# Mirrored weight rows by an indirect gather during the load of x, and by SBUF copies, instead of a reversed copy in DRAM

## The chip, the core and the metric

The kernel runs on one core of one Trainium2 chip. The metric is the device time in microseconds; the kernel before takes 273.87 us in the median of five runs (271.23 to 274.94). The engines of the core are called TensorE (PE; its weight load is PEld), VectorE (DVE), ScalarE (ACT), GpSimd (POOL) and Sync (SP). Sync does no arithmetic: it issues DMAs, in the order of its program.

## What is computed

The input x has 2048 rows of 448 values in bfloat16. Two layers follow one another; each is a global filter (A) and a feed-forward block (B), both with a residual and a layer norm without parameters:

```
def _A_ref(x, w_r, w_i):
    X = rfft2(x.astype(float32), axes=(-2, -1))
    X = X * (w_r + 1j * w_i)              # 2048 x 225 complex weights
    return irfft2(X, s=(S, D)).astype(bfloat16)

def _B_ref(x, w1, b1, w2, b2):
    h = x @ w1 + b1                       # 448 -> 1792
    r = where(h > 0, h, 0)
    return (r * r) @ w2 + b2              # 1792 -> 448

x = x + _A_ref(layernorm(x), A_w_r, A_w_i)
x = x + _B_ref(layernorm(x), B_w1, B_b1, B_w2, B_b2)
x = x + _A_ref(layernorm(x), A_w_r, A_w_i)
x = x + _B_ref(layernorm(x), B_w1, B_b1, B_w2, B_b2)
```

The same filter weights w_r and w_i serve both layers.

## The kernel before

**The filter as matmuls.** x lies in SBUF as 16 tiles of 128 rows (`x_raw`, `x_sb`). The transform over 2048 rows is split into a part over 32 and a part over 64 positions. Stage A (`first_A`, line 774) does the first part, tile by tile: layer norm statistics (`ln_stats`, line 731), a copy of the mirrored second half of x (`xr`, lines 684 to 686), the transform matrix scaled by the inverse deviation (`Fs`), five matmuls, and an evacuation from PSUM to `XA`. All 16 tiles must be through A before the next stage. Then come, over the nine groups of frequencies in `GROUPS` (line 24), four stages: TD (transform along the 448 columns, line 793), evacuated to `U`; B (the 64-part, line 814, with the matrices `G_sb`), evacuated to `EF`; W (the weights, on VectorE, line 829), which writes `Z`; and Bi (the inverse 64-part, line 847, with `H_sb`), evacuated to `VT`. `U`, `EF` and `Z` are parts of the tensor `arena`, and so is `b1r`, where the bias b1 lands. TI and AI are the last inverse parts; they and the feed-forward block follow tile by tile (`ffn`, line 1083).

**The weights in SBUF.** Stage W multiplies by two tensors, `Wa` and `Wb`. They live in the memory of `xin` and `yT`, which hold normalised rows and their transpose during the feed-forward block, so the profile calls them xin and yT. Each has 33 blocks of 225 columns (`WC`) on 128 partitions. Partitions alternate between rows of w_r and rows of w_i; `Wb` has the two parts swapped (`W[i ^ f::2]`). Blocks 0 to 16 are rows of the weights as they lie in DRAM. Blocks 17 to 32 are rows of the other half of the spectrum, in reversed order over the partitions ("mirrored rows"). Stage W of group (1,) needs block 1 and block 32.

**Where the mirrored rows come from.** Lines 676 to 678 copy the upper half of each group of 32 rows, for w_r and for w_i, into a DRAM scratch `Wrev` with the groups reversed, 16 x 64 rows of 450 bytes for each. `load_W` (line 689) loads a range of either tensor: two DMAs for the plain blocks and two from `Wrev` for the mirrored ones. It is called for Wa and Wb, for a first and a second range of frequencies (`RANGES`, line 25), and again at lines 1138 to 1141 for layer 2, since the feed-forward block has overwritten them by then.

**Who orders the work.** All instructions are recorded with modelled costs and then put in order by a list scheduler (`_Sched.schedule`, line 307): each unit has a priority, which is the length of the modelled chain behind it plus a bias from the table `PR` (line 115), by stage, layer and group. The table `EN` (line 116) says which engines an evacuation, a copy or a scaling may run on (a is ScalarE, d VectorE, p GpSimd, the other letters a choice of these); the scheduler takes one. Within a queue the initial DMAs keep the order in which they are recorded (`sch.chain`, line 670). On Sync that is: x in five pieces (line 672), Wrev twice, TD, then for the first range G, Wa, Wb, H, J and b1 (lines 699 to 707), then for the second range G, Wa, Wb and H. Only FA goes by ScalarE's queue (line 671). Then come the late loads (line 710), which wait for one group of `U`: matrices of the last stages, the feed-forward weights, b2. A DMA that waits for an event holds up everything behind it on its queue.

**Small things.** GpSimd clears a part of `Z` (line 683) and writes `ones` (line 679); with `ones` TensorE runs dummy matmuls (line 1147) wherever the scheduler finds gaps[...]. `b1_columns` (line 721) turns b1 into a column with one matmul against `J_sb` and a VectorE copy.

Of the kernel before, what the change touches and what calls it, by code (L numbers as in the profile page):

```python
# [10 lines left out]
P = 128  # L11
# [14 lines left out]
WC = 225  # L26
# [88 lines left out]
PR = {'TD': [[1459729, 1259808, 1256228, -3108200, -3115463, -3359604, -3126041, -3425431, 1074746], [2520683, -882130, 2513278, 1403817, -946609, -1006157, -1079382, -1083072, 1408461]], 'B': [[1237773, 1050720, 1249483, 1207627, -3305020, -3131895, -3380703, -3131879, -3405365], [2513805, -1004943, 1405526, 2514030, 1385417, -1091018, 967616, -1128168, -974908]], 'W': [[1253039, 1078572, 1237053, 1034800, 903280, 1085367, 1237103, 1077859, 864382], [258958, 196705, -32086, -31831, 199273, -68617, -58145, -231565, -289839]], 'Bi': [[-3488292, -3416654, -3131052, 3604675, 3610720, 3611807, 3612729, 3611813, -3301256], [-1103789, 969189, -981009, 1254540, 970491, 1105225, 1552262, 1255862, 1105109]], 'ln': [[923936, 825492, 38979, -60850, -37351, -57698, -179414, -623263, 911016], [-271548, -172641, -867906, -1299696, -1320737, -1236672, -1088818, -1447761, -1447490]], 'TI': [[3619976, 3632657, -3289350, -3332308, 3495818, -3359644, -3382949, -3414332, 3519280], [1261769, 1520394, -1042615, -960154, -1117170, -1090629, 1004310, 1104983, -956137]], 'AI': [[4634856, 3460927, 3455093, 3457451, 3466064, 3457816, 4635449, 4511391, 4582726], [-1052212, 1009347, -1087268, -918268, 922485, 1002479, -1037023, 968706, 962689]], 'xb': [[-9860, 798649, -72029, -73353, -90047, -409254, -607363, -507705, 928714], [-893728, -411180, -1254094, -1698528, -1387951, -1443371, -1673366, -1302405, -1812411]], 'h': [[3487659, 4652010, 4616526, 4619112, 4279252, -3285016, 4657270], [-1019342, 991342, 978381, 984290, -1370620, -1116942, 970059]], 'o': [[4661274, 3474862, 4512632, 4653567, 4636097, 4526347, 4564327, 4535148, 4512085, 4508609, 3950179, 3692114, 3696435, 4495598, 3696450, 3616074], [974079, -1169174, 993521, 1038340, 1009246, 993378, 1005699, -1124270, 998883, -1120813, 996336, -1111884, -1172470, -1092181, 987813, -1358625]], 'A2': [[-72035, 284724, -512615, -580766, 929799, -602369, -46361, -576264, 286964, 286775, 286081, 263197, -46145, 286915, -45242, 261493]], 'A1': [[-779, 1247740, 1250779, 1248346, 1246850, 1247319, 1229425, 1230467]], 'aux': [[1178171, 1361770, 1207975, 1470618]], 'A1x': [[77129, -557721, -161592, 998558, 1237344, 1250337, 1172287, -364362]], 'A1f': [[1236079, 88644, 10154, 1243572, 1069050, 1242682, 1242298, 1245995]], 'A1m': [[1247229, 1244654, 1232513, 1232515, 1232520, 1233784, 1090466, 1090451]], 'A1e': [[91431, 1262114, 1234063, 821447, 1226285, 1050805, 1202378, 1161214]], 'A2f': [[-66167, -58636, -509981, -604863, -46624, -51134, -65898, 91768, -45472, 282466, -800266, 262425, -50208, 187315, -808565, -41160]], 'A2s': [[261559, -869540, -630612, -577929, 87311, -116879, -611112, -5940, 190215, -5765, 140813, 56793, 142295, -803032, 255003, 284498]], 'A2m': [[4542048, 3987428, 3994225, 3994222, 4572260, 3668875, 4538774, 3956827, 3571174, -1111431, 1402630, -891134, -1110561, 1395497, 1402686, 1403856]], 'A2e': [[-590800, 320887, 286230, 188640, -45373, -70277, 332615, 191914, -90624, -52362, 212173, 30004, -86939, 123899, -676333, 212918]], 'TDe': [[1232797, 1033581, 1154642, 1278733, 910181, 1202635, 884503, 865587, 1171272], [234287, 1417255, 495995, 497071, -692296, -708408, 116793, 481473, -31496]], 'Be': [[1200284, 1164674, 1131653, 1169731, 847780, 910804, 858910, 875738, 764326], [-673471, -562228, -700927, 509333, -668554, 482845, -571588, -638456, -610624]], 'Ws': [[1121940, 1017298, 877937, 1032459, 1071284, 902054, 1033802, 894050, 1203015], [212971, -52164, -46639, -245211, -58995, -232137, -245502, -184844, -32998]], 'Bie': [[916036, 852841, 889310, 787021, -7275, 912434, 20519, 815367, 892886], [1425225, 487576, -647465, -980124, -655085, -74395, -74265, -181695, -980116]], 'TIe': [[984358, 928435, 897342, -482262, -48765, -430781, 660660, 817396, 914899], [-281201, -65231, -282303, -289086, -289168, -715848, -279815, -281401, -129383]], 'AIf': [[-3552, -92775, -329502, 40139, 70612, 12525, -118916, -459850, -116926], [-493364, -1130841, -1393844, -459441, -971123, -1107764, -912857, -1318923, -1108227]], 'AIs': [[86761, 782322, 38289, 6120, 64218, -59055, -459688, -181931, 53487], [-268252, -1086758, -871049, -882940, -1366310, -1105429, -921449, -1316086, -1362286]], 'lnq': [[216007, -824667, -30202, -469940, -549631, -29481, 10194, -106170, -63028], [-1301120, -1525322, -1460274, -1354285, -1518321, -1584492, -282120, -1317624, -1311702]], 'lny': [[134655, 81887, 30689, -60625, -63986, -78551, 54758, -622412, -65538], [5687, -408331, -899111, -1240287, -1321630, -1511641, -1102623, -1489541, -1703014]], 'fl': [[3485031, 3484724, -3492741, 4199187, 4682003, 4593201, 4541514, -3167665, 4085732], [-1027343, -1036111, -999372, -1485712, 986133, -1257709, -1086255, 916561, 1055334]], 'fle': [[905334, -49032, 934732, -36098, -136978, -622183, -570281, 25108, -505182], [-306736, -824319, -951824, -1361677, -380305, -946687, -1019748, -866050, -219706]], 'hA': [[-91316, -94830, -804496, -803653, -613427, -30062, -46967], [-269918, -1324305, -1361165, -1320271, -1328874, -1558623, -269889]], 'hD': [[57549, -446183, -809038, -509961, -437101, -809519, -103640], [-906097, -1805974, -1432344, -1761489, -1721726, -1363125, -1284385]], 'oD': [[26793, -111208, -638756, -125186, -585807, -75004, 60726, -67909, -4895, -507284, -62475, -418670, 272545, -37450, -48441, 261019], [-1030248, -948113, -1221985, -1677027, -1690921, -1311510, -1733759, -1579025, -1728934, -1777603, -1665476, -1642112, -1777768, -1724124, -1625446, -1379584]]}  # L115
EN = {'lny': ['baadaaddd', 'bbdababdb'], 'A1x': ['rbrpparp'], 'A1f': ['xxpprqdx'], 'A1e': ['baadbbab'], 'A2s': ['adabbddababaabdd'], 'A2e': ['bdadbaadabbadaaa'], 'TDe': ['abdaaabab', 'abadaaaad'], 'Be': ['abababbab', 'abaaabaaa'], 'Bie': ['bababbbbb', 'aaaaabbda'], 'TIe': ['bdbaabaaa', 'aabaabbba'], 'fle': ['aabdbaddb', 'bdbddbddd']}
# [389 lines left out]
def bass_interleave_layers__spectral_gfnet__dense_activation_squared_relu__prompt_kernel(nc, A_x, A_w_r, A_w_i, B_x, B_w1, B_b1, B_w2, B_b2, out):  # L506
# [4 lines left out]
    sch = _Sched()  # L511

    with ExitStack() as es:
# [152 lines left out]
        out_dram = out.rearrange("b (p t) d -> p (b t) d", t=NT)  # L666
        memset(warm[:, 0:1], 1.0)
# [3 lines left out]
        dma("act", FA_sb[:], dc["FA"])  # L671
        for e, a, b in (("sp", 0, 2), ("sp", 2, 4), ("sp", 4, 8), ("sp", 8, 12), ("sp", 12, 16)):
            dma(e, x_sb[:, a:b, :], x_dram[:, a:b, :], slow=1.5)
        w_dram = [w.rearrange("(q k) l -> q (k l)", k=32) for w in (A_w_r, A_w_i)]
        Wrev = nc.dram_tensor("Wrev", (2, 64, 16 * WC), BF16, kind="Internal").ap()
        for i in range(2):
            dma("sp", Wrev[i].rearrange("q (c e) -> c q e", c=16),
                w_dram[i][::-1, 16 * WC:32 * WC].rearrange("q (c e) -> c q e", c=16), writes=[f"Wrev{i}"], slow=1.5)
        memset(ones[:], 1.0, eng="pool")
        sch.warm_deps = [sch.last_write[k] for k in _pages(ones[:])][:1]  # L680
        sch.warm_from = 1300.0
        sch.cold_until = 8000.0
        memset(Z[:, :, :, LW:256], 0.0, eng="pool")
        for a, b in ((0, 2), (2, 4), (4, 6), (6, 8), (8, 10), (10, 12), (12, 14), (14, 16)):
            at[:] = 0, a // 2
# [13 lines left out]
        for n, (p0, p1) in enumerate(RANGES):  # L699
# [5 lines left out]
            if n == 0:  # L705
                dma("sp", J_sb[:], dc["J"])
                dma("sp", b1r, B_b1.rearrange("(f p) -> f p", p=P))
# [523 lines left out]
```

## Time and profile before

| what | value |
|---|---|
| median of five runs | 273.87 us (271.23 to 274.94) |
| the profiled execution | 270.1 us |
| its span, first to last instruction | 268.3 us |
| granted TensorE clock, mean | 1.000 of full speed |
| first x pieces landed; last x piece landed | 3.5 us; 9.8 us |
| Wrev landed, w_r and w_i | 15.3 and 16.5 us |
| b1 landed | 24.8 us |
| first TD matmul; first W multiplication | 20.9 us; 24.0 us |
| last evacuation of Bi, layer 1 | 45.0 us |
| first TD matmul and last evacuation of Bi, layer 2 | 146.9 us; 168.4 us |

All times in the profile are counted from the start of the span. An instruction row of a timeline reads: start, length, engine, line, operation, output<-inputs, shapes, count, and in brackets how long its engine had been idle before it and what ended that. The chain of waits goes back from the last instruction, at each step to what released it. A row "SPq" is the issue of a DMA on Sync's queue; the time to landing is counted from that issue. In the stretches each engine's busy time is followed by its count of instructions; the DMA share is the mean over the 16 DMA engines and can pass 1 where transfers overlap.

### The profile page before, as it was taken

What the parts mean: (1) busy time and instruction counts of PE and PEld (TensorE: products, weight loads), DVE (VectorE), ACT (ScalarE), POOL (GpSimd) and SP (SyncE); (2) the same over time, 40 slices, a digit from 0 to 9 for tenths busy, and PEclk for the clock granted to TensorE, in tenths of its full rate; (3) what the DMA queues carried; (4) which work ended last, traced back from release to release, by engine and by line L of the source; (5) the groups of instructions that cost most, each with busy time, mean ns of one, the idle gap of its engine ahead of it and who ended that gap; (6) DMA issues with size and microseconds to landing.
All of it is one profiled execution on the core that took longest, in us unless ns stands there. A gap on an engine that the chain in (4) does not pass through costs nothing.

```text
span 268.3 us, 6395 instructions
## 1 busy us (share of the span) xinstructions
PE 256.3 (96%) x2383; PEld 162.1 (60%) x2383; DVE 203.6 (76%) x707; ACT 184.6 (69%) x390; POOL 8.2 (3%) x20
## 2 busy tenths in 40 slices
PE   7987999999999999999999999998999999999996
PEld 2666987686645544445557986775754444554454
DVE  4883896999999998566878999799899755213522
ACT  6875997995886657883647997876979885005700
POOL 2630000000000000000000000000000000000000
PEclk9999999999999999999999999999999999999999
DMA  6999999004932244004000000002233600110011
GB/s 187 219 262 308 401 355 292 4 2 91 175 95 97 42 108 108 2 2 137 1 2 0 2 4 0 4 0 45 55 78 75 98 0 20 34 53 19 0 37 51
DMA packets 26554, 23.25 MB, mean 87 GB/s; under 512 B 18364, under 2 KB 23068, under 8 KB 26396
## 3 DMA queue, kind: packets, MB, share of 16 engines
q1 hardware_dynamic: 26380, 22.78, 31.4%
q8 instruction: 19, 0.31, 0.5%
q10 hardware_dynamic: 144, 0.07, 0.1%
q14 instruction: 11, 0.09, 0.1%
HBM read 17.33 MB, written 2.76 MB: 75 GB/s over the span
## 4 chain that ended last, share of the span: by engine, by line
PE 72%; DMA 9%; ACT 8%; DVE 6%; SPq 3%; issue 1%; DVEq 0%
PE ps L588 72%; DMA Wrev<-in_A_w_i_dram 5%; ACT arena L628 4%; DMA yT<-xin 3%; SPq L583 3%; DVE arena L646 2%; ACT VT L628 1%; DMA arena<-in_B_b_dram 1%; ACT tmp L628 1%; ACT XA L628 1%; DVE tmp L646 1%; DVE xin L655 1%; DVE x_raw L926 0%; DVE st L956 0%; DVE x_raw L928 0%
## 5 line engine op out<-in xcount | busy, mean ns | idle before, releaser
L611 ACT ACTIVATE arena<-ps,b1T 128x512 bf16<-128x512 f32 (+1 forms) x140 | 74.3, 614 | 31.0 <-PE ps L588 30.8
L588 PE MATMUL ps<-yT,W_sb 64*128 64x512 bf16 (+1 forms) x980 | 87.2, 333 | 1.2 <-DMA yT<-xin 0.9
L588 PE MATMUL ps<-W_sb,arena 128*128 128x448 bf16 (+1 forms) x476 | 87.1, 342 | 0.0
L588 PEld LDWEIGHTS ps<-yT,W_sb 64*128 64x128 bf16 x980 | 49.0, 94 | 39.1 <-ACT arena L611 3.7
L588 PEld LDWEIGHTS ps<-W_sb,arena 128*128 128x128 bf16 x476 | 46.0, 98 | 37.4 <-issue 0.8
L646 DVE TENSOR_TENSOR arena<-arena 128x512 bf16<-128x512 bf16 (+1 forms) x140 | 46.9, 365 | 19.1 <-ACT arena L611 19.0
L628 ACT ACTIVATE arena<-ps 128x896 bf16<-128x896 f32 (+1 forms) x33 | 26.5, 893 | 3.9 <-PE ps L588 3.8
L1045 DVE TENSOR_TENSOR x_raw<-ps,arena 128x448 bf16<-128x448 f32 (+1 forms) x23 | 13.3, 580 | 20.8 <-PE ps L588 20.8
L1147 PE MATMUL ps<-ones 128*128 128x512 bf16 x54 | 17.1, 437 | 1.9 <-POOL ones L659 1.9
L628 ACT ACTIVATE VT<-ps 128x512 bf16<-128x512 f32 x29 | 16.7, 661 | 2.4 <-PE ps L588 2.4
L628 ACT ACTIVATE XA<-ps 128x512 bf16<-128x512 f32 x24 | 13.3, 593 | 6.8 <-PE ps L588 6.8
L646 DVE TENSOR_TENSOR arena<-tmp 128x896 bf16<-128x896 bf16 (+1 forms) x32 | 17.2, 587 | 0.2
L588 PE MATMUL ps<-H_sb,arena 128*128 128x128 bf16 x256 | 16.5, 219 | 0.7 <-DVE arena L646 0.4
L728 ACT ACTIVATE VT<-x_raw 128x448 bf16<-128x448 bf16 x24 | 13.7, 576 | 4.9 <-DVE x_raw L928 4.8
L646 DVE TENSOR_TENSOR tmp<-VT 128x224 bf16<-128x224 bf16 (+1 forms) x56 | 16.1, 315 | 0.4
L588 PEld LDWEIGHTS ps<-H_sb,arena 128*128 128x128 bf16 x256 | 14.8, 98 | 2.7 <-DVE arena L646 2.7
L588 PE MATMUL ps<-arena,G_sb 128*128 128x224 bf16 x128 | 14.2, 259 | 0.4 <-ACT arena L628 0.4
L728 ACT ACTIVATE tmp<-x_raw 128x448 bf16<-128x448 bf16 x14 | 8.0, 573 | 8.8 <-DVE x_raw L1041 8.6
L628 ACT ACTIVATE tmp<-ps 128x896 bf16<-128x896 f32 (+1 forms) x16 | 12.6, 853 | 2.0 <-PE ps L588 2.0
L928 DVE SCALAR_TENSOR_TENSOR x_raw<-ps,x_raw 128x448 bf16<-128x448 f32 x24 | 14.0, 614 | 0.0
L588 PEld LDWEIGHTS ps<-arena,G_sb 128*128 128x128 bf16 x128 | 11.9, 98 | 1.4 <-ACT arena L628 1.4
L748 DVE BATCH_NORM_STATS2 st<-x_raw 128x6 f32<-128x448 bf16 (+1 forms) x19 | 10.9, 585 | 0.2 <-DMA x_raw<-in_A_x_dram 0.2
(75 smaller groups left out, 263.1 us busy)
## 6 DMA issues: line engine op xcount, KB each, us to landing
xin<-Wrev SPq DMA_DIRECT2D x8, 225.0 KB, 3.2
yT<-Wrev SPq DMA_DIRECT2D x8, 225.0 KB, 4.4
W_sb<-in_B_w_dram SPq DMA_DIRECT2D x2, 896.0 KB, 11.6
out_dram<-x_raw SPq DMA_DIRECT2D x15, 112.0 KB, 1.7
W_sb<-in_B_w_dram SPq DMA_DIRECT2D x1, 1568.0 KB, 18.2
x_raw<-in_A_x_dram SPq DMA_DIRECT2D x3, 448.0 KB, 6.5
H_sb<-c_H SPq DMA_DIRECT2D x1, 1088.0 KB, 9.4
G_sb<-c_G SPq DMA_DIRECT2D x1, 768.0 KB, 6.5
```

What stands on the lines that cost most here:

```text
L583: return e.dma_start(o, i)
L588: op = sch.add("pe", lambda e: e.matmul(_res(o), lhsT, rhs, start=start, stop=stop, skip_group_check=skip), [lhsT, rhs], [o], cost=max(_fr ...
L611: sch.add("act", lambda e: e.activation(o, _res(i), func, **kw), rd, [o], cost=c)
L628: op = sch.add("act", lambda e: e.activation(o, _res(i), ACT.Copy) if h[0].eng == "act" else e.tensor_copy(o, _res(i)), [i], [o], cost=c[" ...
L646: sch.add(eng, lambda e: e.tensor_tensor(o, _res(a), b, op), [a, b], [o], cost=_free(o) / rate + 69.0)
L655: sch.add(eng, lambda e: e.tensor_scalar(o, i, s1, s2, op0=op0, **kw), rd, [o], cost=_free(o) / 3.84 + 50.0 + (10.0, 80.0, 140.0)[len(rd) ...
L728: sch.add("act", lambda e: e.activation(o, x, ACT.Square, accum_out=sd[:, t, 1:2]), [x], [o, sd[:, t, 1:2]], cost=560.0)
L748: small(lambda e, si=si, xi=xi: e.bn_stats(si, xi), [xi], [si], _free(xi) / 0.96 + 69.0)
L928: small(lambda e, xx=xx, xi=xi, r=r, i=i: e.scalar_tensor_tensor(out=xx, in0=_res(r), scalar=1.0, in1=xi, op0=ALU.mult, op1=ALU.add, accum ...
L1045: sch.add("dve", lambda e: e.tensor_tensor(o, _res(i), xb[:, t, d0:d1], ALU.add), [i, xb[:, t, d0:d1]], [o], cost=(d1 - d0) / 0.96 + 69.0)
L1147: return lambda e: e.matmul(ps[:, b, :], ones[:], ones[:, None, :].to_broadcast([P, 4, P]), start=True, stop=True)
```

## The change

- `Wrev` is no longer written at the start. Instead, GpSimd issues two indirect DMAs, one for w_r and one for w_i, which take 64 rows of 7200 bytes each straight from the weights to all 16 mirrored blocks of Wa. The row numbers 127, 125, ... 1 come from an `iota` on GpSimd (`back`). Both DMAs wait for the first piece of x (tiles 0 and 1).
- In layer 1 Wb's mirrored blocks are copied from Wa, SBUF to SBUF, by four DMAs on Sync, at the places where they were loaded from `Wrev`. Wa's four loads from `Wrev` go.
- After the second H, Sync writes `Wrev` from Wa by two DMAs, in rows of 7200 bytes. Layer 2 loads from it as before.
- b1 and J move from Sync's queue to ScalarE's, right behind FA.
- `ones` is written by VectorE instead of GpSimd.
- The tables `PR` and `EN` are new: every stage of layer 1; in layer 2 all but TD, B, W and Bi with their evacuations. So the order of instructions differs in the whole kernel. The tables are left out below, but for two entries of EN for layer 1's stage A (copies of the mirrored x and the scaling of the transform matrix).

```
-EN = {... 'A1x': ['rbrpparp'], 'A1f': ['xxpprqdx'], ...}
+EN = {... 'A1x': ['brxprrdr'], 'A1f': ['xrpxprbp'], ...}
...
+        back = sb("back", [64, 1], mybir.dt.int32)
+        sch.add("pool", lambda e: e.iota(back[:], [[0, 1]], base=127, channel_multiplier=-2), [], [back[:]], cost=100.0)
...
         dma("act", FA_sb[:], dc["FA"])
+        dma("act", b1r, B_b1.rearrange("(f p) -> f p", p=P))
+        dma("act", J_sb[:], dc["J"])
         for e, a, b in (("sp", 0, 2), ("sp", 2, 4), ("sp", 4, 8), ("sp", 8, 12), ("sp", 12, 16)):
             dma(e, x_sb[:, a:b, :], x_dram[:, a:b, :], slow=1.5)
+        for i in range(2):
+            o = Wa[1 - i::2, 17 * WC + 1:33 * WC + 1]
+            src = A_w_i if i else A_w_r
+            sch.add("pool", lambda e, o=o, src=src: e.indirect_dma_start(
+                o, None, src.rearrange("(q k) l -> q (k l)", k=16), bass.IndirectOffsetOnAxis(back[:, 0:1], 0)),
+                [back[:], x_sb[:, 1, 0:2]], [o], is_dma=True, cost=1200.0, lat=2.0 * 64 * 16 * WC / sch.DMA_RATE)
...
-        for i in range(2):
-            dma("sp", Wrev[i].rearrange("q (c e) -> c q e", c=16),
-                w_dram[i][::-1, 16 * WC:32 * WC].rearrange("q (c e) -> c q e", c=16), writes=[f"Wrev{i}"], slow=1.5)
-        memset(ones[:], 1.0, eng="pool")
+        memset(ones[:], 1.0)
...
-        def load_W(W, f, p0, p1):
+        def load_W(W, f, p0, p1, first):
...
             for i in range(2):
-                dma("sp", W[1 - (i ^ f)::2, WC * (25 - 8 * h) + 1:WC * (33 - 8 * h) + 1],
-                    Wrev[i][:, (8 - 8 * h) * WC:(16 - 8 * h) * WC], reads=[f"Wrev{i}"])
+                c0, c1 = WC * (25 - 8 * h) + 1, WC * (33 - 8 * h) + 1
+                o = W[1 - (i ^ f)::2, c0:c1]
+                if not first:
+                    dma("sp", o, Wrev[i][:, c0 - 17 * WC - 1:c1 - 17 * WC - 1], reads=[f"Wrev{i}"])
+                elif f:
+                    dma("sp", o, Wa[1 - i::2, c0:c1], slow=1.3)
...
-            load_W(Wa, 0, p0, p1)
-            load_W(Wb, 1, p0, p1)
+            load_W(Wa, 0, p0, p1, True)
+            load_W(Wb, 1, p0, p1, True)
             dma("sp", H_sb[:, HQ * (p0 - 1):h1], dc["H"][:, HQ * (p0 - 1):h1])
-            if n == 0:
-                dma("sp", J_sb[:], dc["J"])
-                dma("sp", b1r, B_b1.rearrange("(f p) -> f p", p=P))
+        for i in range(2):
+            dma("sp", Wrev[i], Wa[1 - i::2, 17 * WC + 1:33 * WC + 1], writes=[f"Wrev{i}"])
...
-            load_W(Wb, 1, p0, p1)
-            load_W(Wa, 0, p0, p1)
+            load_W(Wb, 1, p0, p1, False)
+            load_W(Wa, 0, p0, p1, False)
```

## The prediction

> **What bounds the kernel now.** I read, in this order, the page's busy table, the chain that ended last, the busy time by stretches, the Sync queue's timeline, and the timelines of VectorE and GpSimd over the first 45 us. The page first:
>
> ```profile
> span 268.3 us, 6395 instructions
> ...
> PE 256.3 (96%) x2383; PEld 162.1 (60%) x2383; DVE 203.6 (76%) x707; ACT 184.6 (69%) x390; POOL 8.2 (3%) x20
> ...
> L1147 PE MATMUL ps<-ones 128*128 128x512 bf16 x54 | 17.1, 437 | 1.9 <-POOL ones L659 1.9
> ```
>
> TensorE is busy for 256.3 of 268.3 us, but 17.1 us of that is line 1147, the dummy matmuls that keep the clock up. So 268.3 - 256.3 + 17.1 = 29.1 us are not real matmuls, and only a change there can help. By the stretches, 0 to 20.9 holds some 12 us of it, 20.9 to 53.2 some 6, 140 to 192 some 9, the tail the rest. The change touches the first two directly. The chain of waits, in order of time (start, length, what):
>
> ```profile
> 3.81 12.73 DMA Wrev<-in_A_w_i_dram
> 16.54 0.02 issue
> 16.55 0.46 SPq L583
> ...
> 21.33 3.49 DMA arena<-in_B_b_dram
> 24.82 0.05 issue
> 24.87 7.86 PE ps L588 x82
> ```
>
> All that leads up to 24.87 us is a queue: the mirrored copy of w_i into DRAM takes 12.73 us; Sync waits for it before the first load of Wrev; ten more issues stand in line; the last is b1 (the "arena" row), and TensorE, which takes its instructions in order, waits for b1. Behind it the elementwise engines bind (columns: stretch, length, busy PE, PEld, DVE, ACT, POOL, then clock, DMA share, GB/s):
>
> ```profile
> 7.60:16.20 8.60, 8.04 (x65) 5.89 (x64) 7.98 (x34) 7.11 (x20) 5.83 (x12) 1.00 1.17 209
> 20.90:24.90 4.00, 2.49 (x25) 2.26 (x25) 1.69 (x3) 2.00 (x3) 0.00 (x0) 1.00 0.95 324
> 24.90:27.30 2.40, 2.40 (x26) 2.38 (x27) 0.79 (x4) 1.50 (x3) 0.00 (x0) 1.00 0.91 281
> 27.30:43.50 16.20, 15.63 (x201) 14.25 (x199) 15.79 (x30) 15.83 (x25) 0.00 (x0) 1.00 1.03 376
> ```
>
> From 27.3 to 43.5, VectorE and ScalarE are full; before it, from 20.9 to 27.3, VectorE works 2.5 of 6.4 us. VectorE itself (start, length, ..., idle before it):
>
> ```profile
> 23.03 1.09 DVE L629 CAST arena<-ps 128x896 bf16<-128x896 f32 x1 [3.53 <-PE ps L588]
> 24.04 0.38 DVE L646 TENSOR_TENSOR tmp<-arena,xin 128x448 bf16<-128x448 bf16 x1
> 24.34 0.39 DVE L646 TENSOR_TENSOR tmp<-arena,yT 128x448 bf16<-128x448 bf16 x1
> ...
> 27.29 0.63 DVE L646 TENSOR_TENSOR tmp<-arena,xin 128x896 bf16<-128x896 bf16 x1 [1.43 <-ACT arena L628]
> ...
> 32.54 0.63 DVE L646 TENSOR_TENSOR tmp<-arena,yT 128x896 bf16<-128x896 bf16 x1 [0.34 <-DMA yT<-in_A_w_i_dram]
> ```
>
> The weights (xin holds Wa, yT holds Wb) are waited for only once, 0.34 us at 32.54. But issue plus time to landing gives, for single loads: Wb's mirrored rows 18.97 + 4.4 = 23.4, used at 24.34; first H 19.61 + 4.9 = 24.5; second Wb 25.76 + 6.8 = 32.5, used at 32.54; second H 27.70 + 9.4 = 37.1, used from 38.15. The whole transform is planned within about a microsecond of the loads, so moving compute alone earlier would meet them at once.
>
> **The skill.** (1) "DMA: Bandwidth & Descriptors", Specifications, wants 512 B or more per transfer. The trace agrees: between 9.75 and 14.25 us, while the 450-byte rows of Wrev move, the engines carry 126 GB/s at a share of 1.25, against 376 GB/s at 1.03 later. (2) Same page, "Issuing engines are not separate DMA queues": loads from all queues run on the same 16 engines and interleave. So a gather on GpSimd's queue buys no bandwidth, only a place in line; the trace of before has no such DMA. (3) "SBUF — State Buffer", "A bandwidth-pool intuition that's wrong": a DMA issued by GpSimd went from some 620 to 3100 ns beside a VectorE copy, since GpSimd could not write its descriptors meanwhile. The trace of before has no case of it.
>
> **The change part by part.** The sum is against the profiled execution, 270.1 us with span 268.3 (1.8 us around it); the median shown is 273.87, 3.8 above it.
>
> *Removed: Wrev at the start.* Two issues of 0.70 and 0.89 us, Sync's waits of 3.8 and 0.8 us, and about 0.92 MB in 450-byte rows. Also gone are the four loads of Wa from Wrev.
>
> *b1 and J move to ScalarE's queue, behind FA.* Two issues of about 0.37 us (FA's), 0.8 with gaps. ScalarE idled 0.94 us before x came at 3.57, so this is hidden; without that cover 0.8. b1 lands before 10 us instead of 24.82. The PE gap falls away: weight loads stop at 23.13 and resume at 24.86, of which 1.5 to 1.7 us was the wait. ScalarE idles 1.61 and VectorE 1.43 us just behind it for the same reason, and from there both are full. Gain 1.5.
>
> *Order of the first groups.* The next thing late is the first W. The first U is evacuated by 22.0, but B starts at 22.83, behind 20 TD matmuls; in layer 2, where weights are resident, B follows TD by 148.12 - 146.94 = 1.2 us against 1.9 here. Early weights let the new priorities use this: 0 to 0.8, I take 0.7. The wait at 32.54: 0.3. Sum 2.5. As a check, layer 2 does the same stages from first TD to the last evacuation in 168.42 - 146.94 = 21.5 us, layer 1 in 45.04 - 20.92 = 24.1. The difference, 2.6 us, is about all that faster loads can give here, although layer 2's TD matmuls are smaller.
>
> *Added: iota and two gathers on GpSimd.* No such row before. Low end: an estimate of 1 us each to generate, from the first-byte figure in the page's Specifications. They wait for the first x load (3.53), so GpSimd is free at 5.5:
>
> ```profile
> 1.62 0.20 POOL L659 MEMSET ones<- 128x128 bf16 x1
> 6.20 0.55 POOL L640 TENSOR_SCALAR Fs<-FA_sb,rstd 128x256 bf16<-128x256 bf16 x1 [4.38 <-DVE rstd L764]
> 7.66 1.61 POOL L629 COPY VT<-x_raw 128x448 bf16<-128x448 bf16 x3 [0.91 <-DMA x_raw<-in_A_x_dram]
> ```
>
> GpSimd sat idle until 6.20, so iota and gathers hide there. High end: the 3.1 us of (3) for each; two give 3.5 + 6.2 = 9.7. Behind them wait the Fs scalings and mirrored x copies, and behind those TensorE's A matmuls. GpSimd's work from 7.6 to 16.7 is 6.3 of 9.1 us, so 2.8 us of slack ends at about 9; cost 0 to 0.7, I take 0.1. Data: "Anatomy of one DMA" prices 2.0 us + bytes/436 GB/s, or 3.1 us for 461 KB, doubled in its data part beside x; both land at an estimated 10 to 11 us.
>
> *x beside the gathers.* Before, tiles 4 to 7 landed at 1.65 + 6.0 = 7.65, the last x at 2.60 + 7.2 = 9.8, with Wrev's rows among them. Now Wrev's go and 0.92 MB of long rows comes slightly later. VectorE is full from 7.6 to 16.2 (7.98 of 8.6), 6 us beyond the last x, so only tiles 4 to 7 matter: -0.3 to +0.5, I take 0. Ones on VectorE costs nothing: it idles 2.67 us before x.
>
> *Wb copied from Wa.* Sync waits for the gathers in front of these copies; behind them stand H, the second ranges and the late loads, for which Bi on TensorE and W on VectorE wait. The break-even is 15 to 16.5 us, where Sync waited before. At 10 to 11 it is no wait of consequence, since TD, G and 0.69 MB of rows are still moving behind x. By bytes: 3.1 MB at 350 GB/s (between the 324 and 376 above) after x puts first H at about 19 instead of 24.5; then 3.6 MB at 376 puts second H at 29 instead of 37. The SBUF copies have no row of their own; at the 0.6 us issue and 4.4 us of the same load from DRAM they are neutral, at double the bytes (4 x 0.23 MB, 2.5 us) they still leave over 3 us.
>
> *Wrev written afterwards.* 0.92 MB at 376 GB/s is 2.5 us plus two issues, ahead of or among the late loads. These end at about 42 instead of 49.1 (4 MB more), so nothing is late. In layer 2 the same loads of Wrev remain, 5 us and more off the path.
>
> *New priorities and engine choices everywhere.* Line 115's list changes for most stages of both layers, not for layer 2's TD, B, W and Bi. Between 143.4 and 192 us TensorE has 2.8 us idle and 6 us of dummies; nothing in the diff alters a resource there. Bounds -2 to +5; I take 0.
>
> Sum: -1.5 - 0.7 - 0.3 + 0.1 = -2.4, rounded with the check of 2.6 to -2.5. Profiled: 270.1 - 2.5 = 267.6. On the median: 273.87 - 2.5 = 271.4 us.
>
> **Rivals.** *Gathers eat the gain:* generating them holds GpSimd to about 11.5, 2.5 us past its slack, and A ends that much later. For: no evidence of their price here. Against: the slack. Time 273.9. *More is gained:* the new order also takes 3 us out of the 9 in 140 to 192. For: the room exists, with dummies of 2 us in 160 to 165. Against: those stages run at full VectorE and ScalarE. Time 268.4. *Slower, order at an FFN's entry:* TensorE waits for a transposed tile (issue to landing 3.3 and 4.9 us on the chain, yT<-xin) with nothing else in its queue. It decides once over 5.2 us more stands open; two such waits, 8.2, less 2.5, give 279.6. For: at 181.23 one already stands open beside 0.63 us of idle PE. Against: the first layer hides it entirely.
>
> **How the numbers follow.** The forecast (gain 1.5 to 3.5; own range 270.4 to 272.4) gets 0.50, gain eaten 0.20, more gained 0.17, slower 0.13. One per cent, 2.7 us, is about what a measurement can tell from no change. A little over half the forecast (0.26) and all of "more" make faster 0.43; the rest, with the eaten case, same 0.42; the slower case and the tail of the eaten one 0.15. The range runs from 267.2, a little beyond "more gained", to 275.4, the eaten case with 1.5 us more lost; outside it lies chiefly the slower case.
>
> **What would show it.** Right: no PE wait for b1; first W on VectorE by about 22.5 to 23; its full stretch starting near 25 and last evacuation near 42.5; GpSimd's first Fs before 9; gathers landed by 15; H by 20 and 30. Wrong: TD starting after 21.5 (gathers or x), copies of Wb landing after 23, or most of the difference arising after 53 us, which would be the new order and not the loads.

## The result and the profile after

The changed kernel takes 270.2 us in the median (268.72 to 271.88, 26 runs); the kernel before, run beside it, 273.64 us (269.85 to 275.77, 47 runs). The ratio is 0.991, with a 95% interval of 0.989 to 0.993. The medians stand further apart than that, at 0.987, because the ratio leaves out runs more than 1.5% above the fastest of their kernel, and the kernel before spreads over 2.2% by itself (experiment 3 looks into that spread). The forecast was 271.4 us, with an own range of 270.4 to 272.4; the median lies just below that range. The page of the changed kernel:

```profile
span 267.7 us, 6410 instructions
...
PE 256.1 (96%) x2383; PEld 163.2 (61%) x2383; DVE 202.7 (76%) x704; ACT 184.4 (69%) x392; POOL 11.0 (4%) x24
```

The profiled execution takes 269.48 us, against 270.1 before, and the span is 0.6 us shorter. So the two profiled executions differ by much less than the medians. The chain that ended last, in order of time (start, length, what), shows that the first wait is a new one:

```profile
1.12 0.71 ACTq L583
1.86 5.34 DMA J_sb<-c_J
7.20 0.14 issue
7.33 0.18 PE ps L588
7.54 0.17 DVE b1T L650
7.71 0.53 DVE st L758
...
22.78 16.54 PE ps L588 x200
```

The queue behind `Wrev` is gone from the chain. In its place stands J: issued third on ScalarE's queue at 1.86 us, landed at 7.20. The matmul for b1 waits for it, and a copy on VectorE waits for that matmul. VectorE's own timeline (start, length, operation, and in brackets its idle time before) says what hangs on that copy:

```profile
7.54 0.17 DVE L650 COPY b1T<-ps 128x14 f32<-128x14 f32 x1 [6.49 <-PE ps L588]
7.62 0.62 DVE L758 BATCH_NORM_STATS2 st<-x_raw 128x6 f32<-128x448 bf16 x1
...
24.13 1.77 DVE L629 CAST arena<-ps 128x896 bf16<-128x896 f32 x2 [3.10 <-PE ps L588]
25.94 0.39 DVE L646 TENSOR_TENSOR tmp<-arena,xin 128x448 bf16<-128x448 bf16 x1
```

The new order puts b1's copy before the first statistics of x. VectorE works in order, so it is idle from 1.05 to 7.54 us although the first x has landed by 3.6. The first W multiplication comes at 25.94 us, later than before (24.04). What follows is denser. The stretches (length, then busy time of PE, PEld, DVE, ACT, POOL, clock, DMA share, GB/s):

```profile
3.50:7.60 4.10, 0.61 (x3) 0.23 (x3) 0.06 (x1) 2.01 (x8) 2.58 (x3) 1.00 0.87 286
7.60:16.20 8.60, 8.37 (x48) 4.54 (x47) 8.01 (x39) 6.01 (x18) 4.32 (x9) 1.00 0.98 366
...
24.90:27.30 2.40, 2.40 (x28) 2.40 (x26) 2.20 (x6) 2.22 (x4) 0.00 (x0) 1.00 1.00 420
27.30:43.50 16.20, 16.16 (x209) 14.88 (x207) 16.09 (x32) 15.95 (x26) 0.00 (x0) 1.00 0.80 278
```

The first of these stretches in the kernel before:

```profile
3.50:7.60 4.10, 4.10 (x12) 1.55 (x11) 3.22 (x18) 3.38 (x11) 0.55 (x1) 1.00 0.89 271
```

In this stretch VectorE works 0.06 of 4.10 us, where it worked 3.22 before. From 24.9 to 27.3 it works 2.20 of 2.40 (0.79 before), and in the long stretch it is full to within 0.11 us (0.41 before). Most loads also came as forecast: the gathers were issued at 4.42 and 6.26 and landed at 11.5 and 13.1 us, somewhat late; H landed at 17.5 and 27.7, before at 24.5 and 37.1; the last large weights landed near 41.

The whole span splits into five parts that add up. The parts are: start to the first TD matmul; that to the start of layer 1's last Bi evacuation ("filter 1"); that to layer 2's first TD matmul ("FFN 1"); layer 2's filter likewise; and the rest. The kernels in the lower rows are the experiments below.

| kernel | to TD | filter 1 | FFN 1 | filter 2 | rest | span |
|---|---|---|---|---|---|---|
| before | 20.92 | 23.51 | 102.51 | 20.87 | 100.5 | 268.3 |
| after | 22.78 | 21.35 | 102.36 | 20.87 | 100.3 | 267.7 |
| loads only (2a) | 20.35 | 21.57 | 103.68 | 20.87 | 100.3 | 266.8 |
| loads, b1 and J (2b) | 21.19 | 21.58 | 103.66 | 20.87 | 100.4 | 267.7 |
| changed, b1's matmul later (4) | 18.94 | 21.57 | 102.33 | 20.88 | 100.3 | 264.0 |

From before to after, the first part loses 1.86 us and filter 1 gains 2.16. Nothing else moves by more than 0.2.

### The profile page after: what moved, and what is told of

Read it like the earlier page. It is cut to its first block, busy times and chain, and to the rows that moved or that the text cites. A ratio compares the mean times of both kernels' runs of the same rounds, so it can differ in the third digit from the quotient of the medians.

```text
span 267.7 us, 6410 instructions
## 1 busy us (share of the span) xinstructions
PE 256.1 (96%) x2383; PEld 163.2 (61%) x2383; DVE 202.7 (76%) x704; ACT 184.4 (69%) x392; POOL 11.0 (4%) x24
## 3 DMA queue, kind: packets, MB, share of 16 engines
q1 hardware_dynamic: 23968, 21.82, 27.3%
## 4 chain that ended last, share of the span: by engine, by line
PE 76%; ACT 9%; DVE 8%; DMA 4%; issue 1%; ACTq 0%; DVEq 0%
PE ps L588 76%; ACT XA L628 3%; ACT arena L628 3%; DMA J_sb<-c_J 2%; DMA yT<-xin 2%; DVE arena L646 1%; ACT tmp L628 1%; ACT mv L611 1%; DVE st L758 1%; DVE x_raw L936 1%; DVE st L966 1%; DVE tmp L646 1%; ACT VT L628 1%; PE ps L1157 1%; DVE tmp L629 0%
## 5 line engine op out<-in xcount | busy, mean ns | idle before, releaser
L588 PEld LDWEIGHTS ps<-yT,W_sb 64*128 64x128 bf16 x980 | 50.2, 94 | 37.4 <-ACT arena L611 5.1
L646 DVE TENSOR_TENSOR arena<-arena 128x512 bf16<-128x512 bf16 (+1 forms) x140 | 47.9, 366 | 19.1 <-ACT arena L611 18.7
L628 ACT ACTIVATE arena<-ps 128x896 bf16<-128x896 f32 (+1 forms) x32 | 25.6, 909 | 2.5 <-PE ps L588 2.5
L628 ACT ACTIVATE XA<-ps 128x512 bf16<-128x512 f32 x30 | 16.2, 594 | 1.5 <-PE ps L588 1.5
L588 PE MATMUL ps<-arena,G_sb 128*128 128x224 bf16 x128 | 14.3, 259 | 0.1
L628 ACT ACTIVATE tmp<-ps 128x896 bf16<-128x896 f32 (+1 forms) x16 | 12.7, 852 | 2.0 <-PE ps L588 2.0
L611 ACT ACTIVATE mv<-mv,epst 128x2 f32<-128x2 f32 (+1 forms) x31 | 9.0, 299 | 5.4 <-DVE mv L752 4.3
## 6 DMA issues: line engine op xcount, KB each, us to landing
W_sb<-in_B_w_dram SPq DMA_DIRECT2D x1, 1568.0 KB, 13.1
```

The costliest lines, as they stand in the source:

```text
L588: op = sch.add("pe", lambda e: e.matmul(_res(o), lhsT, rhs, start=start, stop=stop, skip_group_check=skip), [lhsT, rhs], [o], cost=max(_fr ...
L611: sch.add("act", lambda e: e.activation(o, _res(i), func, **kw), rd, [o], cost=c)
L628: op = sch.add("act", lambda e: e.activation(o, _res(i), ACT.Copy) if h[0].eng == "act" else e.tensor_copy(o, _res(i)), [i], [o], cost=c[" ...
L646: sch.add(eng, lambda e: e.tensor_tensor(o, _res(a), b, op), [a, b], [o], cost=_free(o) / rate + 69.0)
```

## The experiments

My theory after the result was that the loads do what was forecast, and that the unforecast loss in front of TD is b1's matmul and copy in first place. One rival was that the gathers and their traffic delay x and stage A; another was that the new order, not the loads, brings the gain. In experiments 1, 2 and 5 the scheduler works out its order first, with the loads of the kernel named, and the DMAs are moved or exchanged in the finished lists afterwards. So the compute instructions keep their order, and only the loads differ; on GpSimd an iota and the gathers come or go.

**1. Only b1 and J moved, order of before.** In the finished lists:

```
+        for k in ("J", "b1"):
+            op = HD_[k]
+            sch.ops["sp"].remove(op)
+            op.eng = "act"
+            sch.ops["act"].insert(sch.ops["act"].index(HD_["FA"]) + 1, op)
```

> The kernel before, its compute order frozen; only the loads of J and b1 moved to ScalarE's queue. Queue theory (the time before is set by the line behind Wrev, b1 being its end): the 1.5 us wait of TensorE at 23.1 goes, but Wb at 23.4 and 32.5 and H at 37 stay where they were, so part of it comes back; gain 0.7 to 1.5 us, ratio 0.994 to 0.998. If moving b1 is all that the change does, the ratio is 0.991. If the new order does it all, 1.000.

Measured: 269.46 us in the median against 271.98, ratio 0.994 (0.991 to 0.997), span 267.7 against 268.3. TensorE no longer waits for b1, whose matmul runs at 22.96. VectorE's timeline shows the next wait:

```profile
31.86 0.63 DVE L648 TENSOR_TENSOR tmp<-arena,yT 128x896 bf16<-128x896 bf16 x1 [1.55 <-DMA yT<-in_A_w_i_dram]
```

It is the wait of 0.34 us at 32.54, grown to 1.55. Filter 1 is 43.75 - 20.57 = 23.18 us, only 0.33 shorter than before. With b1 out of the way, the second range of Wb is late at once: of the 1.5 us that the forecast gave to b1 alone, this trace shows little. The median falls by 2.5 us all the same; experiment 3 shows where that comes from.

**2. The loads, order of before.** Kernel 2a has the gathers, the SBUF copies and the late `Wrev`, with b1 and J still on Sync. Kernel 2b has b1 and J moved too.

```
+        sch.ops["pool"][3:3] = gather
...
+                op.fn = lambda e, o=Wb[i::2, c0:c1], s=Wa[1 - i::2, c0:c1]: e.dma_start(o, s)
...
+        sch.ops["sp"][n:n] = write
```

> The kernel before, its compute order frozen; Wrev at the start replaced by the two gathers, the SBUF copies and the late write of Wrev; J and b1 stay in Sync's queue. Queue theory: the whole queue moves up by 5 us or more, b1 lands near 15 and is waited for no more; gain 2 to 3 us, ratio 0.989 to 0.993. If moving b1 is what matters: the same as with b1 on ScalarE's queue, within 0.5 us. If the new order does it all: 1.000.

> The kernel before, its compute order frozen; all loads as in the changed kernel (gathers, SBUF copies, late Wrev, J and b1 on ScalarE's queue). Queue theory: nothing more than with the gathers alone, within 0.5 us, since b1 was in time there; TD starts near 20.9 and not 22.8, since b1's matmul keeps its late place in the order, so it is as fast as the changed kernel or faster: ratio 0.985 to 0.991. If the new order carries the gain: 1.000.

Measured: 2a takes 268.99 us, ratio 0.991 (0.987 to 0.994), and 2b 269.14, ratio 0.991 (0.988 to 0.994). Filter 1 is 21.57 and 21.58 us, so the loads alone give the whole shortening of that part. TD starts at 20.35 in 2a, not later than before (20.92), so the gathers don't hold it up. GpSimd's timeline of 2a:

```profile
4.39 1.10 POOL L1164 DMA_INDIRECT xin<-in_A_w_r_dram,back  x1 [2.41 <-DMA x_raw<-in_A_x_dram]
5.79 0.89 POOL L1164 DMA_INDIRECT xin<-in_A_w_i_dram,back  x1 [0.30 <-issue]
6.73 0.49 POOL L642 TENSOR_SCALAR Fs<-FA_sb,rstd 128x256 bf16<-128x256 bf16 x1
```

Both gathers are generated before 6.7 us, and the first `Fs`, which ran at 6.20 before, runs at 6.73. But 1.2 us of the gain are lost again in FFN 1. TensorE's timeline of 2a in the first groups of tiles of the feed-forward block, and below it the row of the kernel before:

```profile
63.15 5.64 PE L590 MATMUL ps<-yT,W_sb 64*128 64x256 bf16 x98 [0.75 <-DMA yT<-xin]
69.29 7.08 PE L590 MATMUL ps<-yT,W_sb 64*128 64x512 bf16 x64 [0.51 <-DMA yT<-xin]
```

```profile
70.63 9.67 PE L588 MATMUL ps<-yT,W_sb 64*128 64x512 bf16 x88 [0.15 <-DMA yT<-xin]
```

TensorE waits twice for a transposed tile, 1.26 us together, where the kernel before waits 0.15 us once. As I read it, the old order fits the old loads: when filter 1 ends earlier, less work is left there to cover the transposes. No run changes this place alone. It is the wait of the third rival ("order at an FFN's entry"), though it costs 1.26 us here and not 8.2.

**3. The kernel before, twice more, with a profile.** There is no edit.

> The kernel before, unchanged, profiled again, since its profiled execution (270.1 us) is shorter than its median. Queue theory: where this one takes longer, Wrev's landing (15.3 and 16.5 us in the first profile) and with it b1's (24.8) come later by about the difference, and the rest of the kernel keeps its length. Rival: Wrev and b1 land as before and the difference lies after 53 us.

> The same once more, for a second value: the time against the landing of Wrev and b1 should lie on one line with the other profiles if the queue sets the time.

Measured: 270.99 and 274.0 us. TensorE's row for b1 in the first and in the second:

```profile
25.80 0.18 PE L588 MATMUL ps<-J_sb,arena 14*128 14x14 bf16 x1 [2.05 <-DMA arena<-in_B_b_dram]
```

```profile
26.96 0.18 PE L588 MATMUL ps<-J_sb,arena 14*128 14x14 bf16 x1 [3.63 <-DMA arena<-in_B_b_dram]
```

TD starts at 21.29 and 20.87, but b1 holds TensorE until 25.80 and 26.96; in the profile that the forecast was made from it was 24.87. In the first, b1 and the last Bi evacuation (45.36 instead of 44.43) both come 0.93 us later, and the span is 0.9 us longer: the queue explains it whole. In the second, the copy of w_i into `Wrev` took 13.7 us instead of 12.73 and b1 came 2.1 us later, but the last Bi evacuation started at 47.71, 3.3 us later, and the span is 3.9 us longer. So the three don't lie on one line, as they would if the queue alone set the time. The page of the second shows what came on top (granted TensorE clock in tenths, in 40 slices of the span):

```profile
PEclk9999799999999999999999999999999999999999
```

In the fifth slice the clock is lower: it is 0.50 from 27.5 to 30.9 us, just behind the wait of 3.63 us, and 1.00 after. The executions without a profile agree. In the session of experiments 1 and 2, the mean granted clock was 1.000 in 18 of 40 executions of the kernel before, with a median of 269.96 us, and 0.994 in 21, with 272.58. Of the 47 executions of the kernels 1, 2a and 2b, in which TensorE doesn't wait for b1, none is listed below 0.999; 22 of them are of kernel 1, where nothing but b1 and J has moved. So the wait for b1 costs twice: by its length, and in about half of the executions there by the lower clock behind it. The 2.6 us between the two medians hold both, since a longer wait may go with the lower clock. Against the 18 executions at full clock, the kernels 1, 2a and 2b are only 0.5, 1.0 and 0.8 us faster; the rest of their gain in the medians shows only against executions with the lower clock. From what length a wait brings it is not shown: the waits of 1.49 and 2.05 us in the other two profiles went without it.

So the profile of before was one of the kernel's short executions, at full clock. That, I infer, makes up most of the 2.8 us by which the change moves the medians more than it moves the profiles.

**4. The changed kernel with b1's matmul later.** The matmul waits for the first group of `U`, and the scheduler orders anew; in the traces, apart from the dummy matmuls, only this matmul and its copy change their place.

```
-            mm(q[lambda b: ps[:, b, 0:FB]], b1r, J_sb[0:FB, P - FB:P][:, ::-1], True, True)
+            op = mm(q[lambda b: ps[:, b, 0:FB]], b1r, J_sb[0:FB, P - FB:P][:, ::-1], True, True)
+            for k in _pages(U[:, 1, 0:2]):
+                op.deps.append(sch.last_write[k])
+                op.gdeps.append(sch.last_write[k])
...
+                if first and n == 0:
+                    rank("aux", 0, 0)
+                    b1_columns()
...
-        rank("aux", 0, 0)
-        b1_columns()
```

> The changed kernel with b1's matmul placed after the first TD matmuls instead of ahead of stage A. If VectorE's wait for b1 (until 7.54 us) is what starts stage A late: statistics begin near 3.6, TD starts near 21, 1.5 to 1.9 us less than the changed kernel, ratio to the kernel before 0.984 to 0.986. If x beside the gathers, or GpSimd busy with them, is what delays stage A: TD stays at 22.8, ratio 0.991.

Measured: 265.77 us (265.55 to 266.56) against 271.98, ratio 0.979 (0.974 to 0.984). That is more than I expected, and it beats both kernels. TensorE's timeline:

```profile
18.94 2.08 PE L588 MATMUL ps<-TD_sb,XA 128*128 128x224 bf16 x20 [0.30 <-ACT XA L628]
20.95 0.18 PE L588 MATMUL ps<-J_sb,arena 14*128 14x14 bf16 x1
```

b1's matmul now runs between two TD groups and waits for nothing. TD starts 3.84 us before that of the changed kernel, and the span is 3.7 us shorter. The stretch 3.50 to 7.60 shows where the time was:

```profile
3.50:7.60 4.10, 3.31 (x18) 1.68 (x17) 3.39 (x19) 3.28 (x13) 2.63 (x4) 1.00 0.86 279
```

VectorE works 3.39 of 4.10 us here, against 0.06 in the changed kernel. The median of the kernel before was 271.98 to 274.5 from one chip and hour to another, so I ran the changed kernel and this one once more beside each other.

> The changed kernel once more, as the partner of the kernel with b1's matmul behind the first TD matmuls, on one chip. My theory (the b1 matmul in first place costs stage A's start over 3 us): this one is at 0.985 to 0.993 of the kernel before, and 1.2 to 1.5% slower than its partner. Rival (the partner's lead came from the drift of the kernel before between chips and hours): within 0.5% of its partner.

> The changed kernel with b1's matmul behind the first 20 TD matmuls, once more. My theory: 0.973 to 0.981 of the kernel before; TD starts near 19, the span is near 264, 3.5 us under its partner's. Rival: within 0.5% of its partner.

Measured: 270.4 us (269.62 to 270.77) and 265.95 us (265.14 to 266.07), ratios 0.986 (0.982 to 0.990) and 0.969 (0.965 to 0.972) to a kernel before of 274.5. TD starts at 23.69 and 19.13, and the spans are 267.8 and 264.3. The later matmul is worth 4.4 us in the medians, 1.6%, and no run of one kernel reaches a run of the other. The second ratio is a little better than I expected.

**5. The same kernel with the old loads.** Its compute order is kept, `Wrev` is written at the start again, and Wa and Wb are loaded from it, without gathers; b1 and J stay on ScalarE's queue.

```
+        sp[n:n] = old
...
+                a = _Op("sp", lambda e, o=Wa[1 - i::2, c0:c1], s=src: e.dma_start(o, s), True, 0.0, 0.0)
+                a.deps = [old[i]]
```

> The version with b1 late, its compute order frozen, but with the old loads: Wrev copied in DRAM at the start, all mirrored rows loaded from it, no gathers (J and b1 stay on ScalarE's queue). Queue theory: TD still starts near 19, but W waits for Wb's second range near 32 and Bi for H near 37; the last evacuation of Bi comes near 43.5 instead of 40.5, ratio to the kernel before 0.988 to 0.993. If the new order alone makes b1-late fast, it stays at 0.979.

Measured: 270.71 us against 274.29, ratio 0.988 (0.984 to 0.993); span 269.0. The groups of waits (what waits for what: us in total, times, longest):

```profile
PE ps L589 <- DMA G_sb<-c_G: 2.9, 1, 2.9
```

TD starts at 19.01, as in experiment 4, but the last Bi evacuation starts at 45.55 instead of 40.51. Late loads cost 2.9 us for the second part of G, for which TensorE waits until 28.85, and VectorE waits 1.7 us for Wb's mirrored rows from `Wrev`. From the end of the wait for G on the clock is 0.50 again, from 28.8 to 32.2 us, which takes part in the five microseconds too. So in the traces all that the short stage A gives is lost again without the early loads (268.3 before). The median is still 3.6 us below that of the kernel before, whose executions beside it, but for one of eleven, were at a clock of 0.994 or less.

**6. The changed kernel with J ahead of FA on ScalarE's queue.** Its compute order is kept; only these two issues change places.

```
+        q = sch.ops["act"]
+        a, b = q.index(FA_op), q.index(J_op)
+        q[a], q[b] = J_op, FA_op
```

> The changed kernel, order frozen, with J first and FA last on ScalarE's queue. If VectorE's wait at the start is for J's landing (7.2 us): J lands near 3.2, statistics begin near 4; FA lands later (6 to 7) and the first scaling waits a little; TD starts at 19.5 to 21, ratio 0.981 to 0.986. If b1's own load or the gathers hold stage A, TD stays at 22.8 and the ratio at 0.991.

Measured: 268.65 us against 274.29, ratio 0.980 (0.976 to 0.984); TD starts at 22.22, so the expected 19.5 to 21 was missed. VectorE's timeline:

```profile
4.00 0.17 DVE L650 COPY b1T<-ps 128x14 f32<-128x14 f32 x1 [2.96 <-PE ps L588]
4.09 0.62 DVE L758 BATCH_NORM_STATS2 st<-x_raw 128x6 f32<-128x448 bf16 x1
...
8.42 0.48 DVE L640 TENSOR_SCALAR Fs<-FA_sb,rstd 128x256 bf16<-128x256 bf16 x2 [1.67 <-DMA FA_sb<-c_FA]
```

J landed 2.2 us after issue and the statistics began at 4.09, as wanted. But FA, now third, landed only at about 8.4, and the first `Fs` waits for it. TensorE idles for 1.89 us until 8.85, and from 10.1 to 13.5 us it gets only half its clock, in the middle of stage A; the one execution of six at full clock took 267.24 us, the others 268.58 to 268.94. So how much of the miss is FA's and how much the clock's is open. The third load on that queue, J or FA, landed 5.3 to 6.5 us after its issue, beside the pieces of x, and both are needed at the start.

## Why the prediction was right, point by point

The total was right, and in part by luck: two terms were wrong by almost 4 us each in opposite directions, and the median fell by 3.4 us where the profiled execution, on which the sum was made, fell by 0.6. What holds as forecast is the gain from the loads.

- **Queue behind `Wrev`, order of the first groups, wait at 32.54: -2.5.** Right as a sum. With the loads alone (2a), filter 1 ends 44.43 - 41.92 = 2.5 us earlier. Right also that loads set this part: filter 1 is 21.35 us after the change, and layer 2's filter, with resident weights, 20.87. The single terms are not separable as I priced them: b1 alone shortens filter 1 by 0.33 us in the traces, because the next load is late by then. That the wait for b1 also brings a lower clock in about half of the executions is not in the forecast at all.
- **Gathers on GpSimd: +0.1, landing at 10 to 11 us.** The cost is right: 1.10 and 0.89 us, close to the estimate of 1 us each, with TD no later. The high end, the 3.1 us of "SBUF — State Buffer", did not occur, though VectorE worked 1.89 of the 2.29 us between 4.39 and 6.68 in kernel 2a; no run here shows that wait. The landing was late: from the formula in "DMA: Bandwidth & Descriptors", "Anatomy of one DMA", I had an estimate of 3.1 us, doubled in its data part beside x; 6.8 to 7.5 us after issue were measured. That is below the break-even at 15 us, so it cost nothing.
- **Copies of Wb, late `Wrev`, H at 19 and 29, late loads at 42.** Right: 17.5, 27.7 and about 41; no wait for any of them is on the chain.
- **"ScalarE idled 0.94 us before x came at 3.57, so this is hidden".** This step failed. It counted the issues on ScalarE and the landing, and not the reader. ScalarE did start on x at 3.64, as I had worked out. But the two instructions that read b1 and J moved as well: the matmul to first place on TensorE behind six dummies, the copy to first place on VectorE, ahead of the statistics. Behind them stood stage A. The cost, by experiment 4, is 3.7 us of span and 4.4 us of median. The prediction did name the sign ("TD starting after 21.5"); it started at 22.78, and I had named gathers or x as the cause. Signs of being right were missed for the same late start: first W at 25.94 instead of 23, GpSimd's first `Fs` at 11.39 instead of before 9, the last evacuation at 44.7 instead of 42.5. With b1's matmul later (experiment 4) they are 22.31, 7.54 and 41.1. The move without the new order (2b against 2a) costs 0.84 us before TD in the traces, but 0.15 us in the medians, so this part stays unsettled.
- **New priorities: 0, between -2 and +5.** Mis-sized, and the argument for 0 looked in the wrong place. I looked between 143 and 192 us, where nothing changed (filter 2 is 20.87 in all). With b1's matmul out of the way, the tables (and `ones` on VectorE) bring 3.4 us in the medians (269.14 to 265.77), and the traces place them: 21.19 - 18.94 = 2.25 us in stage A and 103.66 - 102.33 = 1.33 us in FFN 1, about the 1.24 us for which 2b waits for transposes (0.87 and 0.37) and kernel 4 does not. Which of the tables' entries shortens stage A was not tried. The tables also put b1 first, so their net effect is near 0, as forecast, for a reason that I had not seen.
- **The sum on the median.** 273.87 - 2.5 used a profile of 270.1. That one was a short execution at full clock: its wait for b1 was 1.5 to 1.7 us, and two others had 2.05 and 3.63, the last with the lower clock behind it. That the median fell by 3.4 us and the profile by 0.6 agrees with this; the clocks of the executions of before behind the 273.64 us are not on record.
- **A reading.** The 6 us without real matmuls that I read between 20.9 and 53.2 us are 5.3 by the stretches (2.97 idle, 2.35 dummies). No term rests on it.

From trace to trace (single executions, and the kernels follow one another, so the sum closes by itself): the loads bring -1.5 us of span (-2.5 to the end of filter 1, and about 1 given back after it), b1 and J on the other queue +0.9, the tables -3.7, b1 in first place +3.7, together -0.6. Of the rivals, "gathers eat the gain" is ruled out by 2a. "More is gained" was wrong in its place, between 140 and 192 us. The FFN's entry did open, but only under the old order and by 1.26 us.

## What to carry to other kernels

When a load is moved, look for the instructions that read it and at their place in each engine's order: one tiny matmul and copy, ready late and placed first, held VectorE for 6.5 us, some 4 of them with x already there. A change of loads and a change of order should be costed together and tested apart, since an old order fits old loads and gives part of a gain back. Where a long queue decides the end, one profile is one draw of its length; profile the kernel before two or three times before a gain of 1% is priced from it. And look at the granted clock behind a wait of TensorE: here some 2 us of the gain in the medians of experiments 1 and 2 show only against executions with the lower clock.

## What the runs showed of the hardware

- A small load on ScalarE's queue, beside the pieces of x on Sync's, took the longer the later it stood: J, 32 KB, landed 2.2 us after issue as the first DMA on ScalarE's queue, 3.1 us on Sync at 14.3 us, and 5.3 to 6.3 us behind FA and b1. FA, 64 KB, took 2.4 to 2.6 us as the first and about 6.5 as the third. That fits the Trainium skill, "DMA: Bandwidth & Descriptors", "Issuing engines are not separate DMA queues": they interleave on the same 16 engines.
- An indirect gather of 64 rows of 7200 bytes takes GpSimd 0.89 to 1.10 us and lands 6.8 to 7.5 us after issue beside x.
- The issue of b1 on 14 partitions took ScalarE 0.71 us, about twice FA's 0.37.
- The same copy of 0.46 MB between two places in DRAM, in rows of 450 bytes, took 12.7 to 13.7 us from one execution to the next.
- In three of the twelve traced executions TensorE got half its clock for 3.4 us in the course of the first layer's filter: from 27.5 us behind a wait of 3.63 us that ended at 26.96, from 28.8 at the end of one of 2.95 that ended at 28.85, from 10.1 behind one of 1.89 that ended at 8.85. One such stretch makes the mean clock of the execution 0.994 (3.4 x 0.5 of 267 to 272 us); without the wait for b1, 47 of 47 executions were at 0.999 or 1.000, with it 18 of 40.
